# Stores of the activated values moved from ScalarE to SyncE, and the weight and factor work of two MLP stages placed anew

## The chip, the cores and the metric

One core of a Trainium2 chip runs the whole program. The metric is the device time of one execution in microseconds. Engines are called PE (TensorE), DVE (VectorE), ACT (ScalarE), POOL (GpSimd) and SP (SyncE); SP issues DMAs and computes nothing. ACT can issue DMAs too, in its own order of instructions.

## The reference

Attention with a summed key-value product, then a gated MLP with RMS norm, then a second MLP, all in float32:

```python
q_s = softmax(q, axis=-1); k_s = softmax(k, axis=2)       # 8 x 8 heads, 576 x 64
kv = einsum('bhsd,bhse->bhde', k_s, v)
x = einsum('bhsd,bhde->bhse', q_s, kv)                    # as 4608 x 512
xn = x / rms * rms_g
x = (silu(xn @ w_gate) * (xn @ w_val)) @ w_out            # 512 -> 1536 -> 512
h = x @ w_in                                              # 512 -> 2048
return (h * sigmoid(1.702 * h)) @ w_out2                  # 2048 -> 512
```

The weights arrive as 64-bit floats and are decoded to float32 on the chip.

## The kernel before

Every product runs as three matmuls: both operands are split into a rounded part and the rest (a copy on ACT, then a subtraction on DVE or POOL), and high x high, high x low and low x high are summed (`PASSES`, line 488).

The order of all instructions is written out by hand (`tc.manual_schedule()`, line 729). Each engine works its own list in that order, and the semaphores that order the engines among themselves are derived from the tiles: who writes a tile waits for the readers of what stood in that buffer before. A pool with `bufs=n` has n buffers per tag.

**GLU stage** (to line 863). Nine tiles of 512 tokens, 36 slots each. A slot is one product of 12 matmuls: gate, value, output, in turn for 12 blocks. Small jobs hang at slots. In the last tile `todo` (lines 803 to 820) is a list of (earliest slot, job), of which up to three are done per slot (line 856): the weight sets 0 to 3 of the next stage are loaded, summed and split, then the first unit's tokens are loaded (`x2_load`), summed and split. The four accumulators are evicted at the end by ACT through the `ev` tiles (`store_x2`, line 528).

**Input stage** (lines 866 to 921). The second MLP runs each product in seven instead of eight block products: sums of blocks are formed first (`sums`, line 548), each of the seven operands p is split, and the seven products are combined. A unit is 768 tokens; there are six (`NUNIT`), `END` is the last. A unit has four rounds (`in_round`, line 617) over two weight sets each, and a round has seven passes p in `ORDER` (1, 6, 2, 7, 5, 4, 3), a pass being 2 x 6 matmuls of 384 columns. So a unit has 28 passes, counted 0 to 27 from its start; `put2(i, t, fn)` hangs a job behind pass t of unit i, and `put_set(i, t, steps, lag, each)` hangs the load of a weight set at t, its sums at t + lag and its seven splits, `each` per pass, from t + lag + 1. PSUM has 8 banks; a round uses three per set. p = 2 goes into the bank of p = 1 and must wait until ACT has copied p = 1 out (`c1`, line 649); p = 7 and 4 go into the bank of p = 6, p = 3 into that of p = 5, and the additions on DVE (lines 652, 657, 661) must come between. After its addition each result passes through `gelu` (line 623): an activation on ACT into one of 12 `h` tiles, and a store to DRAM, issued by ACT (line 625).

Beside the products of unit 0 the sets 4 to 7 are prepared, all through the one tile `aside`, 5 passes apart (line 889). In units 0 to 4 the next unit's tokens are loaded into the two `raw` tiles (passes 10 and 12), summed (16 and 18) and split in two halves of channels c for each p (passes 20 to 27, lines 891 to 901). The factors of the last two p (4 and 3) have single buffers (`xg`, 4 tiles), the other ten come out of 12 `xf` tiles. In the last unit the sets 0 to 5 of the output weights are prepared in the `raw` tiles (line 902).

**Output stage** (lines 924 to 1015). Nine groups g of 512 tokens by eight sets m; step k = 8 g + m. A step is 42 matmuls of 256 columns into seven banks, p in the order 1, 6, 7, 5, 3, 4, 2. Its operand `uf` is loaded (`u2_load(k + 6)`), summed (`u2_sums`) and split (`u2_split(k + 2)`: a copy on ACT of 1792 columns, the sums of k + 3 and the subtraction on DVE) some steps ahead. Sets 6 and 7 are prepared through the single tile `y` at k = 0 to 2 and 4 to 6 (line 942), with the sums on POOL. In the last step of a group the seven banks are combined into `y` through the tiles `d1`, `d2`, `d3` (lines 986 to 1006), and ACT issues the stores at the next step (`store_out`, line 670).

The buffers of a stage lie where those of the stage before lay, and a new tile waits for the old ones under it (`reuse_waits="tile"`).

Of the kernel before, what the change touches and what calls it, by code (L numbers as in the profile page):

```python
# [8 lines left out]
F32 = mybir.dt.float32  # L9
# [11 lines left out]
def attention_glu_mlp(  # L21
# [595 lines left out]
    def in_round(i, q, after):  # L617
# [5 lines left out]
        def gelu(m, k, dst, src):  # L623
            nc.scalar.activation(dst, src, AF.Gelu_apprx_sigmoid)  # L624
            nc.scalar.dma_start(out=u2_d[i][m][:, k], in_=dst)  # L625
# [44 lines left out]
    def store_out(first, y):  # L670

        done = 0
        while done < P:
            b, o = divmod(first + done, S)
            rows = sum(halves_of(b), [])
            while o >= size(rows[0]):
                o -= size(rows.pop(0))
            m = min(P - done, size(rows[0]) - o)
            if rows[0] < R - 1:
                dst = out[b * S : b * S + FULL].rearrange("(p r) e -> r p e", p=P)[rows[0]]  # L680
            else:
                dst = out[b * S + FULL : (b + 1) * S]
            nc.scalar.dma_start(out=dst[o : o + m, :], in_=y[done : done + m, :])
            done += m
# [44 lines left out]
    with tc.manual_schedule():  # L729
# [74 lines left out]
        for j in range(NTILE):  # L804
            if j + 1 == NTILE:
# [16 lines left out]
            for slot in range(SLOTS):  # L822
# [49 lines left out]
        for p in ORDER[5:]:  # L872
            for c in range(2):
                x2_split(0, p, c)
# [14 lines left out]
        for n in range(4):  # L889
            put_set(0, 5 * n, weight_steps("2i", 4 + n, nc.gpsimd, aside_tile), 2, 3)  # L890
        for i in range(END):
            for c in range(2):
                put2(i, 10 + 2 * c, lambda i=i, c=c: x2_load(i + 1, c))
                put2(
                    i, 16 + 2 * c,
                    lambda i=i, c=c: sums(xraw2[i + 1, c], "B", (nc.vector,) * 4),
                )

            for p, t in zip(ORDER, (20, 21, 22, 23, 24, 26, 27)):
                for c in range(2):  # L900
                    put2(i, t, lambda i=i, p=p, c=c: x2_split(i + 1, p, c))
        for m, t in enumerate((1, 3, 10, 13, 17, 20)):
            put_set(END, t, weight_steps("2o", m, nc.gpsimd), (5, 6, 3, 3, 3, 3)[m])
        put2(END, 0, lambda: u2_load(0))
        put2(END, 18, lambda: u2_sums(0))
        put2(END, 25, lambda: u2_load(1))
# [5 lines left out]
        put2(END, 25, free_x)  # L912
        put2(END, 26, lambda: u2_split(0))
# [14 lines left out]
        def y_tile():  # L928
            return dpool.tile([P, 8, Q], F32, tag="y", bufs=1, name="y")

        for k in range(2, 4):
            u2_load(k)
        for t in sorted(t for i, t in beside):
            for fn in beside.pop((END, t)):
                fn()
# [4 lines left out]

        work = {}
        for m, k in ((6, 0), (7, 4)):
            a = weight_steps("2o", m, nc.gpsimd, y_tile, nc.gpsimd)
            work[k], work[k + 1], work[k + 2] = a[:1], a[1:5], a[5:]
        stores = []
        for k in range(NT // T * NSET):
# [16 lines left out]
            if last:  # L963
# [3 lines left out]
                c1, u2, u3 = (  # L967
                    dpool.tile([P, 512], F32, tag=n, bufs=1, name=n) for n in ("d1", "d2", "d3")
                )
            for p in (1, 6, 7, 5, 3, 4, 2):  # L970
# [19 lines left out]
                if p == 1:  # L990
                    nc.scalar.activation(c1, t, AF.Copy)
                elif p == 6:
                    add(half(u2), half(c1))
                elif p == 7:
                    add(half(u3), half(u2))
                elif p == 5:
                    add(y2[:, :, 0:Q], half(u3))
                    add(half(u2), half(u2))
                    u2_split(k + 2)
                    u2_load(k + 6)  # L1000
                elif p == 3:
                    add(y1[:, :, 0:Q], half(u2))
                elif p == 4:
                    add(y2[:, :, Q:T], half(u3))
                else:
                    add(y1[:, :, Q:T], half(c1))
            if last:
                for i in range(2):
                    for h, y in ((0, y2), (1, y1)):
                        stores.append(  # L1010
                            lambda i=i, h=h, y=y, g=g: store_out(first_token(g, i, h)[2], y[:, i, :])
                        )
# [45 lines left out]
```

## Time and profile before

| | |
|---|---|
| median of 3 runs | 1845.46 us (1845.21 to 1847.75) |
| the profiled execution | 1846.57 us, of which the span from first to last instruction is 1844.8 |
| PE, PEld | 1748.1 us (95%), 1545.6 us (84%) |
| DVE | 1197.5 us (65%) |
| ACT | 781.7 us (42%) |
| POOL | 388.8 us (21%) |
| granted TensorE clock | 0.985 of full speed on the mean |
| DMA | 186.30 MB, 101 GB/s on the mean |

PEld is the loading of weights into TensorE, beside the matmuls. The granted clock of a stretch is a share of 2.4 GHz; the clock has two levels, 1.2 and 2.4 GHz, so 0.92 is a mixture. Input stage and output stage run from 1086 to 1460 and from 1463 to 1838 us. The row of a timeline gives the start, the length, the engine and line, the number of instructions merged, and in brackets how long the engine stood before them and what ended that.

### The profile page before, as it was taken

What the parts mean: (1) busy time and instruction counts of PE and PEld (TensorE: products, weight loads), DVE (VectorE), ACT (ScalarE), POOL (GpSimd) and SP (SyncE); (2) the same over time, 40 slices, a digit from 0 to 9 for tenths busy, and PEclk for the clock granted to TensorE, in tenths of its full rate; (3) what the DMA queues carried; (4) which work ended last, traced back from release to release, by engine and by line L of the source; (5) the groups of instructions that cost most, each with busy time, mean ns of one, the idle gap of its engine ahead of it and who ended that gap; (6) DMA issues with size and microseconds to landing.
All of it is one profiled execution on the core that took longest, in us unless ns stands there. A gap on an engine that the chain in (4) does not pass through costs nothing.

```text
span 1844.8 us, 26565 instructions
## 1 busy us (share of the span) xinstructions
PE 1748.1 (95%) x10092; PEld 1545.6 (84%) x10092; DVE 1197.5 (65%) x2021; ACT 781.7 (42%) x1304; POOL 388.8 (21%) x360
## 2 busy tenths in 40 slices
PE   5777899999999999999999998999999899999998
PEld 4555788888888888888888888999999889999998
DVE  7999875766757567564324355455545877777775
ACT  4565544444435444443212344344435533333332
POOL 4666512121121121211111613000001540000000
PEclk9898999999999999999999999999999999999999
DMA  5344332332223323120001124443343544444442
GB/s 156 120 141 123 115 97 71 96 88 79 75 69 96 90 78 109 35 81 1 23 1 46 32 100 141 137 138 133 110 155 137 177 131 135 136 126 126 128 125 80
DMA packets 201744, 186.30 MB, mean 101 GB/s; under 512 B 58256, under 2 KB 183184, under 8 KB 201616
## 3 DMA queue, kind: packets, MB, share of 16 engines
q1 hardware_dynamic: 163536, 127.96, 23.3%
q10 hardware_dynamic: 38080, 56.64, 8.6%
q8 instruction: 79, 1.29, 0.3%
q14 instruction: 49, 0.40, 0.1%
HBM read 119.54 MB, written 65.01 MB: 100 GB/s over the span
## 4 chain that ended last, share of the span: by engine, by line
PE 77%; DVE 10%; ACT 4%; issue 3%; DMA 2%; ACTq 1%; SPq 1%; POOL 1%; DVEq 0%; POOLq 0%
PE ps_gv L493 29%; PE ps_out L975 19%; PE ps_acc L493 15%; PE ps_in L639 11%; ACT h L624 2%; ACTq L625 1%; PE ps_att L370 1%; ACT xf L553 1%; PE ps_att L399 1%; DVE h L661 1%; DVE w L151 1%; DVE raw L550 1%; DVE raw L151 1%; DVE xf L554 1%; DVE u L509 1%
## 5 line engine op out<-in xcount | busy, mean ns | idle before, releaser
L975 PE MATMUL ps_out<-w2o,uf 128*128 128x256 f32 x3024 | 368.3, 285 | 9.1 <-POOL w2o L554 4.3
L975 PEld LDWEIGHTS ps_out<-w2o,uf 128*128 128x128 f32 x3024 | 367.0, 194 | 10.5 <-POOL w2o L554 4.8
L639 PE MATMUL ps_in<-xf,w2i 128*128 128x384 f32 x2016 | 357.4, 337 | 19.0 <-ACT h L649 12.8
L639 PEld LDWEIGHTS ps_in<-xf,w2i 128*128 128x128 f32 x2016 | 351.9, 189 | 24.6 <-ACT h L649 16.2
L493 PE MATMUL ps_acc<-u,wo 128*128 128x512 f32 x1296 | 327.6, 402 | 7.2 <-POOL wo L161 6.3
L493 PE MATMUL ps_gv<-xs,wg 128*128 128x512 f32 x1296 | 322.3, 397 | 7.7 <-POOL wg L161 6.2
L493 PE MATMUL ps_gv<-xs,wv 128*128 128x512 f32 x1296 | 318.1, 394 | 0.0
L493 PEld LDWEIGHTS ps_gv<-xs,wg 128*128 128x128 f32 x1296 | 243.3, 190 | 63.1 <-POOL wg L161 8.3
L493 PEld LDWEIGHTS ps_acc<-u,wo 128*128 128x128 f32 x1296 | 243.8, 193 | 60.4 <-POOL wo L161 7.6
L493 PEld LDWEIGHTS ps_gv<-xs,wv 128*128 128x128 f32 x1296 | 240.4, 189 | 48.1 <-POOL wv L161 0.8
L161 POOL TENSOR_TENSOR wo<-raw,wo 128x512 fp32r<-128x512 f32 x108 | 142.2, 1317 | 494.5 <-ACT wo L160 476.5
L827 ACT ACTIVATE s<-ps_gv 128x512 f32<-128x512 f32 x108 | 64.6, 598 | 428.6 <-PE ps_gv L493 428.5
L833 DVE TENSOR_TENSOR s<-s,ps_gv 128x512 f32<-128x512 f32 x108 | 73.9, 684 | 203.4 <-PE ps_gv L493 185.5
L624 ACT ACTIVATE h<-h 128x384 f32<-128x384 f32 x144 | 75.6, 525 | 136.6 <-DVE h L661 118.3
L157 POOL TENSOR_TENSOR w<-w,stage 128x512 int32<-128x512 int32 x56 | 73.5, 1313 | 220.1 <-DVE w L154 70.9
L550 DVE TENSOR_TENSOR raw<-raw 128x256 f32<-128x256 f32 (+1 forms) x236 | 106.8, 494 | 10.7 <-DMA raw<-w2d 6.8
L661 DVE TENSOR_TENSOR h<-h,ps_in 128x384 f32<-128x384 f32 x144 | 76.7, 552 | 41.4 <-PE ps_in L639 40.0
L719 ACT ACTIVATE uf<-raw 128x1792 fp32r<-128x1792 f32 x36 | 61.1, 1701 | 84.4 <-PE ps_out L975 61.9
L554 POOL TENSOR_TENSOR w2o<-raw,w2o 128x256 fp32r<-128x256 f32 x42 | 32.7, 808 | 286.2 <-ACT w2o L553 283.5
L721 DVE TENSOR_TENSOR uf<-raw,uf 128x1792 fp32r<-128x1792 f32 x36 | 73.4, 2038 | 19.0 <-ACT uf L719 18.9
L510 DVE TENSOR_TENSOR u<-s,u 128x512 fp32r<-128x512 f32 x108 | 83.2, 770 | 3.7
L360 DVE TENSOR_REDUCE qs<-qe 128x10 f32<-128x640 f32 x32 | 26.2, 820 | 84.8 <-ACT qe L354 84.7
(138 smaller groups left out, 1843.1 us busy)
## 6 DMA issues: line engine op xcount, KB each, us to landing
u<-h ACTq DMA_DIRECT2D x192, 192.0 KB, 1.9
stage<-in_moe_w_out_dram SPq DMA_DIRECT2D x28, 512.0 KB, 3.6
raw<-u SPq DMA_DIRECT2D x24, 512.0 KB, 4.3
x<-ev ACTq DMA_DIRECT2D x36, 256.0 KB, 2.0
stage<-in_moe_w_in_dram SPq DMA_DIRECT2D x16, 512.0 KB, 3.6
w2d<-w SPq DMA_DIRECT2D x32, 256.0 KB, 3.4
out_dram<-y ACTq DMA_DIRECT2D x32, 256.0 KB, 4.1
v_sb<-in_v_dram SPq DMA_DIRECT2D x60, 128.0 KB, 3.1
```

The lines of the kernel that those rows point to most:

```text
L157: return lambda: nc.gpsimd.tensor_tensor(dst, dst, lo, op=ALU.add)
L161: nc.gpsimd.tensor_tensor(dst[:, 1, :], src, f(dst[:, 0, :]), op=ALU.subtract)
L493: nc.tensor.matmul(t, w(a), x(e), start=first and i == 0, stop=last and i == 2)
L510: nc.vector.tensor_tensor(u[:, 1, :], s, f(u[:, 0, :]), op=ALU.subtract)
L550: engine.tensor_tensor(raw[:, o], raw[:, a], raw[:, b], op=op)
L624: nc.scalar.activation(dst, src, AF.Gelu_apprx_sigmoid)
L639: nc.tensor.matmul(t, w[:, a, s, c * P : (c + 1) * P], xfac[i, p, c][:, e, :], start=p in (1, 6, 5) and c == 0 and k == 0, stop=c == 1 and ...
L661: nc.vector.tensor_tensor(v, v, t, op=ALU.add)
L721: nc.vector.tensor_tensor(w[:, 1], raw, f(w[:, 0]), op=ALU.subtract)
L827: nc.scalar.activation(s, tg, AF.Silu)
L833: nc.vector.tensor_tensor(s, s, tv, op=ALU.mult)
L975: nc.tensor.matmul(t[:, i * Q : (i + 1) * Q], u[:, a, LEFT[p] - 1, i * P : (i + 1) * P], w[:, e, m % 2, :], start=m == 0 and i == 0 and n ...
```

## The change

It has these parts:

- The store in `gelu` is issued by SP.
- End of the GLU stage: both pairs of weight sets and the first unit's sums come two to three slots earlier, and from slot 33 on two jobs are done per slot. The splits of p = 4 and 3 for unit 0 no longer stand ahead of the input stage.
- Four PSUM tiles that nothing uses are allocated before the first round, so that it begins with the fifth bank.
- Sets 4 and 6 go through `aside`, sets 5 and 7 through the `raw` tiles, with other passes for load, sums and splits.
- The splits of p = 4 and 3 move from passes 26 and 27 of a unit to passes 0 and 2 of the next.
- In the last unit set 2 goes through `aside`, the passes of all six sets change, u2_load(0) moves from pass 0 to 16, and the first `uf` split from pass 26 to the front of pass 25, without the sums of the next one.
- Output stage: two `y` tiles; the loads of sets 6 and 7 are issued at its start. The tiles `d1` to `d3` are replaced by quarters of `y`. The stores of a group go out in another order, and those of the last group partly on SP, the `y2` half two additions earlier.

```diff
         def gelu(m, k, dst, src):
             nc.scalar.activation(dst, src, AF.Gelu_apprx_sigmoid)
-            nc.scalar.dma_start(out=u2_d[i][m][:, k], in_=dst)
+            nc.sync.dma_start(out=u2_d[i][m][:, k], in_=dst)
...
-    def store_out(first, y):
+    def store_out(first, y, queue=nc.scalar):
...
-    def u2_split(k):
+    def u2_split(k, ahead=True):
...
         nc.scalar.activation(w[:, 0], raw, AF.Copy)
-        u2_sums(k + 1)
+        if ahead:
+            u2_sums(k + 1)
...
-                for q, gate in enumerate((12, 22)):
+                for q, gate in enumerate((10, 20)):
...
-                    todo.append((31, lambda c=c: sums(xraw2[0, c], "B", (nc.vector,) * 4)))
+                    todo.append((28, lambda c=c: sums(xraw2[0, c], "B", (nc.vector,) * 4)))
...
-                for _ in range(3):
+                for _ in range(3 if slot < 33 else 2):
...
-        for p in ORDER[5:]:
-            for c in range(2):
-                x2_split(0, p, c)
+        for _ in range(4):
+            pools["ps"].tile([P, 512], F32, tag="bank", bufs=8, name="ps_none")
...
-        for n in range(4):
-            put_set(0, 5 * n, weight_steps("2i", 4 + n, nc.gpsimd, aside_tile), 2, 3)
-        for i in range(END):
...
+        put_set(0, 0, weight_steps("2i", 4, nc.gpsimd, aside_tile), 2)
+        put_set(0, 3, weight_steps("2i", 5, nc.gpsimd))
+        put_set(0, 6, weight_steps("2i", 6, nc.gpsimd, aside_tile), 4)
+        put_set(0, 4, weight_steps("2i", 7, nc.gpsimd), 9)
+        for i in range(-1, END):
+            if i >= 0:
                 for c in range(2):
+                    t = 10 + (7 if i == 0 else 2) * c
+                    put2(i, t, lambda i=i, c=c: x2_load(i + 1, c))
+                    t = 16 + (4 if i == 0 else 2) * c
...
+            for p, t in zip(ORDER, (20, 21, 22, 23, 24, 28, 30)):
+                for c in range(2):
+                    if t >= 28:
+                        put2(i + 1, t - 28, lambda i=i, p=p, c=c: x2_split(i + 1, p, c))
+                    elif i >= 0:
+                        put2(i, t, lambda i=i, p=p, c=c: x2_split(i + 1, p, c))
+        last = [weight_steps("2o", m, nc.gpsimd, aside_tile if m == 2 else raw_tile) for m in range(6)]
+        for m, load, t in ((0, 1, 6), (1, 3, 9), (2, 1, 12), (3, 10, 15), (4, 13, 19), (5, 18, 22)):
+            put_set(END, load, last[m], t - load)
+        put2(END, 16, lambda: u2_load(0))
+        put2(END, 21, lambda: u2_sums(0))
+        put2(END, 23, lambda: u2_load(1))
...
-        put2(END, 25, free_x)
-        put2(END, 26, lambda: u2_split(0))
+        beside[END, 25].insert(0, free_x)
+        beside[END, 25].insert(1, lambda: u2_split(0, False))
+        put2(END, 25, lambda: u2_load(2))
...
-            return dpool.tile([P, 8, Q], F32, tag="y", bufs=1, name="y")
+            return dpool.tile([P, 8, Q], F32, tag="y", bufs=2, name="y")
...
+        u2_load(3)
+        work = {}
+        for m, k in ((6, 1), (7, 3)):
+            a = weight_steps("2o", m, nc.gpsimd, y_tile, nc.gpsimd)
+            a[0]()
+            work[k], work[k + 1] = a[1:5], a[5:]
...
-                c1, u2, u3 = (
-                    dpool.tile([P, 512], F32, tag=n, bufs=1, name=n) for n in ("d1", "d2", "d3")
-                )
+                c1, u2, u3 = y1[:, :, Q:T], y1[:, :, 0:Q], y2[:, :, Q:T]
+                end = g == NT // T - 1
...
                 elif p == 4:
-                    add(y2[:, :, Q:T], half(u3))
+                    add(u3, u3)
+                    if end:
+                        for i in range(2):
+                            store_out(first_token(g, i, 0)[2], y2[:, i, :], nc.sync)
...
+                for h, y in ((0, y2), (1, y1)):
+                    for i in range(2):
+                        if h or not end:
+                            queue = nc.sync if end and i else nc.scalar
...
```

## Rows read from the trace of the kernel before

**Rows 1.** Busy time by stretch, instructions, granted TensorE clock, DMA share.

```profile
1086.22:1108.86 22.64, 22.63 (x120) 22.31 (x120) 9.60 (x20) 11.72 (x25) 5.74 (x8) 0.92 0.40 136
1223.72:1284.29 60.57, 58.92 (x336) 58.15 (x336) 31.86 (x63) 26.17 (x55) 0.00 (x0) 1.00 0.38 131
1465.50:1502.66 37.16, 37.06 (x293) 36.66 (x293) 30.36 (x45) 15.42 (x17) 11.37 (x13) 0.96 0.55 169
1520.00:1837.64 317.64, 317.63 (x2643) 317.25 (x2641) 243.01 (x356) 107.97 (x69) 0.00 (x0) 1.00 0.40 123
```

**Rows 2.** Waits of PE, 1083 to 1163.5: total, times, longest.

```profile
PE ps_in L639 <- ACT h L649: 6.2, 3, 2.7
PE ps_in L639 <- ACT ev L530: 2.4, 1, 2.4
PE ps_in L639 <- DVE h L661: 2.4, 1, 2.4
PE ps_in L639 <- DVE h L652: 1.4, 1, 1.4
```

**Rows 3.** Timeline of PE: start, us, what, count, idle before and releaser.

```profile
1080.40 0.47 PE L493 MATMUL ps_acc<-u,wo 128*128 128x512 f32 x1 [0.69 <-DVE u L509]
1144.48 16.41 PE L639 MATMUL ps_in<-xf,w2i 128*128 128x384 f32 x84 [2.68 <-ACT h L649]
...
1163.18 58.90 PE L639 MATMUL ps_in<-xf,w2i 128*128 128x384 f32 x336 [2.29 <-ACT h L649]
1223.72 58.92 PE L639 MATMUL ps_in<-xf,w2i 128*128 128x384 f32 x336 [1.65 <-ACT h L649]
...
1463.44 0.50 PE L975 MATMUL ps_out<-w2o,uf 128*128 128x256 f32 x2 [3.18 <-ACT uf L719]
1465.50 37.16 PE L975 MATMUL ps_out<-w2o,uf 128*128 128x256 f32 x293 [1.56 <-DVE uf L721]
1505.14 2.05 PE L975 MATMUL ps_out<-w2o,uf 128*128 128x256 f32 x12 [2.47 <-POOL w2o L554]
1508.99 328.65 PE L975 MATMUL ps_out<-w2o,uf 128*128 128x256 f32 x2717 [1.80 <-POOL w2o L554]
```

**Rows 4.** Stores of line 625: issue min/median/max in ns; landing.

```profile
L625 ACTq DMA_DIRECT2D u<-h x192: 325/326/1175, 1093.8 to 1467.4; - x192
...
DMA to landing us min/median/max: 1.8/1.9/5.8
```

**Rows 5.** x2 loads: issues, KB, us to landing; twelve on SP's timeline.

```profile
raw<-x SPq DMA_DIRECT2D x16, 192.0 KB, 3.5
...
1162.96 6.75 SPq L606 DMA_DIRECT2D raw<-x  x12
```

**Rows 6.** Timeline of ACT, a gelu in unit 5.

```profile
1411.69 0.53 ACT L624 ACTIVATE h<-h 128x384 f32<-128x384 f32 x1 [3.02 <-DMA u<-h]
```

**Rows 7.** Timeline of DVE, the sums of set 5 in unit 0.

```profile
1108.16 1.56 DVE L550 TENSOR_TENSOR aside<-aside 128x256 f32<-128x256 f32 x4 [4.96 <-POOL w2i L554]
```

**Rows 8.** Timeline of ACT across the start of unit 3.

```profile
1282.93 0.94 ACT L553 ACTIVATE xf<-raw 128x384 fp32r<-128x384 f32 x2 [0.40 <-PE ps_in L639]
1283.77 0.85 ACT L649 ACTIVATE h<-ps_in 128x384 f32<-128x384 f32 x2
```

**Rows 9.** Timelines of ACT and DVE at the change of stage.

```profile
1461.71 1.68 ACT L719 ACTIVATE uf<-aside 128x1792 fp32r<-128x1792 f32 x1
...
1463.42 2.02 DVE L721 TENSOR_TENSOR uf<-aside,uf 128x1792 fp32r<-128x1792 f32 x1 [0.26 <-ACT uf L719]
1465.37 1.01 DVE L661 TENSOR_TENSOR h<-h,ps_in 128x384 f32<-128x384 f32 x2
1466.29 3.02 DVE L550 TENSOR_TENSOR raw<-raw 128x256 f32<-128x256 f32 x8
```

**Rows 10.** Timeline of POOL, the sums of set 6.

```profile
1480.16 2.95 POOL L550 TENSOR_TENSOR y<-y 128x256 f32<-128x256 f32 x4 [17.28 <-DMA y<-w2d]
```

**Rows 11.** Timeline of all engines, the last stores.

```profile
1838.42 2.79 ACTq L683 DMA_DIRECT2D out_dram<-y  x5
```

More of the change, by code (lines that the diff above doesn't have):

```diff
@@ L682, in store_out @@
                 dst = out[b * S + FULL : (b + 1) * S]
-            nc.scalar.dma_start(out=dst[o : o + m, :], in_=y[done : done + m, :])
+            queue.dma_start(out=dst[o : o + m, :], in_=y[done : done + m, :])
             done += m
@@ L887, in put_set @@
                 put2(i, t + lag + 1 + n // each, fn)
-        for n in range(4):
-            put_set(0, 5 * n, weight_steps("2i", 4 + n, nc.gpsimd, aside_tile), 2, 3)
-        for i in range(END):
[L892 to L896, printed above, removed]
-                )
-            for p, t in zip(ORDER, (20, 21, 22, 23, 24, 26, 27)):
-                for c in range(2):
[L901 to L906, printed above, removed]
+        put_set(0, 0, weight_steps("2i", 4, nc.gpsimd, aside_tile), 2)
[4 more added lines that the diff above has]
+            if i >= 0:
+                for c in range(2):
+                    t = 10 + (7 if i == 0 else 2) * c
+                    put2(i, t, lambda i=i, c=c: x2_load(i + 1, c))
+                    t = 16 + (4 if i == 0 else 2) * c
+                    put2(
+                        i, t, lambda i=i, c=c: sums(xraw2[i + 1, c], "B", (nc.vector,) * 4)
+                    )
+            for p, t in zip(ORDER, (20, 21, 22, 23, 24, 28, 30)):
[10 more added lines that the diff above has]
+        put2(END, 23, lambda: u2_load(1))
         def free_x():
@@ L928, in y_tile @@
         def y_tile():
-            return dpool.tile([P, 8, Q], F32, tag="y", bufs=1, name="y")
[L931 to L935, printed above, removed]
+            return dpool.tile([P, 8, Q], F32, tag="y", bufs=2, name="y")
+        assert not beside
+        u2_load(3)
[4 more added lines that the diff above has]
+            work[k], work[k + 1] = a[1:5], a[5:]
         u2_sums(1)
@@ L939, in attention_glu_mlp @@
             u2_load(k)
[L941 to L944, printed above, removed]
         stores = []
@@ L990, in attention_glu_mlp @@
                 if p == 1:
-                    nc.scalar.activation(c1, t, AF.Copy)
+                    nc.scalar.activation(c1, half(t), AF.Copy)
                 elif p == 6:
-                    add(half(u2), half(c1))
+                    add(u2, c1)
                 elif p == 7:
-                    add(half(u3), half(u2))
+                    add(u3, u2)
                 elif p == 5:
-                    add(y2[:, :, 0:Q], half(u3))
-                    add(half(u2), half(u2))
+                    add(y2[:, :, 0:Q], u3)
+                    add(u2, u2)
                     u2_split(k + 2)
@@ L1001, in attention_glu_mlp @@
                 elif p == 3:
-                    add(y1[:, :, 0:Q], half(u2))
+                    add(u2, u2)
                 elif p == 4:
-                    add(y2[:, :, Q:T], half(u3))
+                    add(u3, u3)
+                    if end:
+                        for i in range(2):
+                            store_out(first_token(g, i, 0)[2], y2[:, i, :], nc.sync)
                 else:
-                    add(y1[:, :, Q:T], half(c1))
+                    add(c1, c1)
             if last:
[L1008 to L1012, printed above, removed]
+                for h, y in ((0, y2), (1, y1)):
+                    for i in range(2):
+                        if h or not end:
+                            queue = nc.sync if end and i else nc.scalar
+                            stores.append(
+                                lambda i=i, h=h, y=y, g=g, queue=queue: store_out(
+                                    first_token(g, i, h)[2], y[:, i, :], queue
+                                )
+                            )
         for fn in stores:
```

1 line of the change is left out of this document (removed).

## The prediction

> **What bounds the kernel now.** I read the busy time by stretch first [rows 1]. PE is busy in nearly all of a steady unit of the input stage (58.92 of 60.57 us) and in all of the output stage after 1520. There 336 matmuls of 384 columns take 58.92 us, 0.175 us each, and 2643 matmuls of 256 columns take 317.63 us, 0.120 each, 5.04 for the 42 of a set. The change leaves those 2016 and 3024 matmuls as they are, so 353 + 363 us of PE stay, and what can move is the time in which PE stands or runs slowly. Then the waits of PE in the first unit [rows 2] and its timeline [rows 3] show where. Of the stretches in [rows 1] the one from 1086.22 has a granted clock of 0.92 and the one from 1465.5 of 0.96, a mixture of the levels 2.4 and 1.2 GHz; each starts right behind a gap. The price of that is in the same rows: 120 matmuls took 22.64 instead of 21.0 us (1.6 lost), 293 took 37.16 instead of 35.2 (2.0 lost).
>
> What PE loses from 1080 on:
> - (a) 0.69 us at 1080, waiting for a u split on DVE [rows 3];
> - (b) 2.42 us for the last eviction (ev) before the input stage [rows 2], and 1.6 of slow clock behind it;
> - (c) in unit 0, 2.4 and 1.4 us for DVE and 6.2 for the copy of line 649, of which 2.29 are unit 1's start [rows 2, 3]: 7.7. The 84 matmuls from 1144.48 took 16.41 instead of 14.7 us, 1.7 more. 9.4;
> - (d) at the starts of units 1 to 5, 2.29, three times 1.65, and 1.64 [rows 3] (of four alike the first stands there): 8.9;
> - (e) at the change of stage 3.18 and 1.56 us for uf, with two matmuls between, and 2.0 of slow clock: 7.0;
> - (f) before set 7, 2.47 and 1.80 for w2o on POOL; the 12 matmuls between took 2.05 instead of 1.4, and the 2717 behind took 328.65 instead of 326.0, so 2.6 + 0.6: 7.5;
> - (g) the tail behind the last matmul.
>
> **The change part by part.**
>
> *Stores on SyncE.* ACT issues 192 stores of 0.326 us [rows 4]; they go, 63 us of ACT time, 2.6 per round of 14.7. Little of it is on the path by itself: only at unit starts, in unit 0 and at the change of stage does PE wait for ACT. They now stand in SP's order, each behind its gelu and behind every load that the program puts before it. SP's own time is small: 32 stores by 0.33 and twelve x2 loads by 6.75 [rows 5] are 17 us in a unit of 60. The new cost is the head of the queue. A gelu that writes a new h tile takes the one allocated twelve before it, whose gelu and store stood about four passes (8.4 us) earlier. Less the gelu (0.53), the issue (0.33) and the landing (1.9 [rows 4]) 5.6 us are to spare. Six loads of one x2 half take 3.4 us to issue and 3.5 to land [rows 5], so a store right behind them may come up to 1.3 us too late; a store issued two passes later doesn't. The nearest row is a gelu that stood 3.02 us for a store in unit 5, where no PE gap follows [rows 6]; so I take nothing. The ends are 0 and the whole landing, 3.5 us in each of the 11 rounds that hold loads (three in unit 0, one in each of units 1 to 4, four in unit 5). They can't be below nothing, as the ACT time gained is counted in the other terms.
>
> The Trainium skill speaks against this part: "DMA: Bandwidth & Descriptors", section "Anatomy of one DMA", says that DMA engines don't wait on semaphores, the issuing sequencer does, before dispatch. By that a load that waits for its tile holds all stores behind it. The trace agrees [rows 7]: the load of set 5 wasn't issued until POOL was done. By the gelu of [rows 6] the sum below stays as it is; by the rule at its hardest, 11 landings of 3.5, all of it would be gone.
>
> *Last factors in the next unit (d).* Ahead of the copies of line 649, which must free the first bank before p = 2, ACT now has four xf splits of 0.47 and eight issues in the last round; the first copy ends 1.65 us after PE wants the bank [rows 3, 8]. After the change no split and no issue stands there: 0.94 for the last two splits and 2 x 0.33 come off at the very end, and the earlier two as much again, 3.2 against the 1.65 to 2.29 needed. The splits go behind the copies of the next unit, five passes (10 us) before their use for p = 4. Rounds inside a unit, which have that order, show no gap (336 matmuls in one piece [rows 3]). I take all 8.9; low end 5.
>
> *Banks and sums at the end of the GLU stage (a, b).* Sums three slots (8 us) earlier leave DVE free before the last u: 0.7 gained. PE's first matmul waited for the last eviction, so the first banks are those of the accumulators; with four stepped over the first round starts in others, and 2.42 and the slow clock behind it go, 4.0. Its x2 factors are ready; only p = 4 and p = 3 come later. Low end 0.
>
> *Rooms for sets 4 to 7 (c).* Today one tile serves four sets: DVE stands 4.96 us before the sums of set 5, because the load waited for POOL to finish set 4 [rows 7], and PE waits for DVE and ACT behind it. After it, sets 5 and 7 load into the x2 tiles from pass 3 and 4 on; their sums stand at 6 and 13, set 6's at 10, all three to nine passes (6 to 19 us) behind the load, for about 3.5 us of landing. What is late next is set 4: its load waits for the ev stores as before while PE starts 2.4 us sooner. Counted from PE's new start, the last ev ends at 2.4, its store lands at 4.6 (0.33 + 1.9), the load at 8.1 (3.5); sums (1.5 [rows 9]), two xf halves and the u3 add (0.5 each) end at 11.1, and PE wants that bank at five passes, 10.5: 0.7 lost. 9.4 - 0.7 = 8.7; low end 4.
>
> *Change of stage (e).* The first uf split moves one pass up. Count from PE's end of p = 5 in the last round: ACT finishes its gelus at 1.2 and uf (1.68) at 2.9, DVE's half (2.02) at 4.9 [rows 9]. PE ends p = 4 and 3 at 4.2 and stands 0.5 for the low half. DVE then has four adds (2.2), the sums of two ufs (3.0) and uf 1 (2.0): ready at 12.1, while PE wants it at 4.7 + 5.04 = 9.8. That is a new gap of 2.3 at set 1. Loss 2.8 instead of 7.0: 4.2 gained; ends 2.2 (the slow clock returns) and 7.0.
>
> *Sets 6 and 7 (f).* POOL stood 17.28 us until y was loaded [rows 10], and set 7 had to wait for set 6's tile. With two y tiles both loads are issued at the start, the sums of set 7 stand at k = 3 and it is used at k = 7, 20 us later; POOL, idle for those 17.28 us today, has 3.0 of sums and seven splits to do for each. 7.5 gained; low end 3.
>
> *Partial sums in y, stores of the tail (g).* The adds stay as many and as long; no gap stands there now, nothing gained or lost. In the last group the y2 stores go out on SP two adds earlier and the y1 stores on two queues. Five issues on ACT took 2.79 us at the end [rows 11]; now one or two do: 1.3 gained, ends 0 and 2.2.
>
> **Sum.** 0.7 + 4.0 + 8.7 + 8.9 + 4.2 + 7.5 + 1.3 = 35.3 us. The profiled execution took 1846.57 us (span 1844.8 and 1.8 around it): 1811.3. The median of before is 1.1 below it, so 1810.
>
> **The rivals.**
> 1. *Stores late by what exceeds the slack.* 1.3 us for each of the ten x2 halves, 13 us: 1823. For it: the 5.6 us are worked out without the data of the loads in front; against it: of the stores close behind loads only those of p = 3 are wanted again so soon, and [rows 6].
> 2. *The change doesn't remove the waits of unit 0 and the stage change fully.* DVE, whose sums stood 4.96 us for a load [rows 7], stays the last in unit 0 and keeps half of (c), and the short gaps that stay keep the clock low (1.6 + 1.7 + 2.0): 4.7 + 5.3 = 10 us, 1820. For it: the slow stretches all begin behind gaps of 2.4 us or more, and I forecast one of 2.3.
> 3. *Slower: the queue of SP becomes the bound.* In each of the 11 rounds with loads the gelus wait for stores that stand behind loads, PE stands for a landing (3.5) and pays 1.7 of slow clock: 11 x 5.2 = 57, and 35.3 gained: 1867. It decides from 3.2 us a round on. Against it: 17 us of SP's 60 per unit.
>
> **How the numbers follow.** Forecast 0.66 (own range 1806 to 1817), rival 1 0.13, rival 2 0.13, rival 3 0.06; 0.02 lie between, near no change. The likeliest gives 1810. With every best end the sum is 0.7 + 4.0 + 9.4 + 8.9 + 7.0 + 7.5 + 2.2 = 39.7, 1805.8. From 1805 to 1825 the range takes in rivals 1 and 2. Faster by over 0.2% (3.7 us, about what a measurement of this kernel can tell from no change) 0.92, within 0.02, slower 0.06.
>
> **What would show it.** PE's timeline without a gap at the five unit starts (d) and none before set 7 (f); the input stage starting within 0.3 us of the last output matmul of the GLU stage (b); gaps in unit 0 that sum to about 1 us with a granted clock of 1.00 (c); one gap of about 2 us at set 1 of the output stage (e). Wrong: gelus that wait for u<-h, PE waiting for ACT or DVE right behind pass 10 or 12 of a unit, or a granted clock under 1.00 in the units.

## The result, and the profile after

The changed kernel takes 1816.07 us (median of 4 runs, 1815.13 to 1816.74) beside 1845.34 us before: 0.984 of the time, with a 95% interval of 0.982 to 0.986. The forecast was 1810, the range 1805 to 1825. Its profiled execution took 1816.74 us (span 1814.9), 29.9 us of span less than before where 35.3 were forecast. The time lies in the range. The sum came out 5.4 us too large, and its terms missed by more than that in both directions. Of all runs one, of the last experiment, took 1936.97 us at a granted clock of 0.85, and no time below counts it.

PE's timeline of the kernel after, the same view as [rows 3], from the last products of the GLU stage to the last matmul:

```profile
1077.64 5.60 PE L493 MATMUL ps_acc<-u,wo 128*128 128x512 f32 x24
1085.66 349.92 PE L639 MATMUL ps_in<-xf,w2i 128*128 128x384 f32 x2016 [2.42 <-ACT ev L530]
1435.42 0.40 PE L984 MATMUL ps_out<-w2o,uf 128*128 128x256 f32 x2
1436.33 5.56 PE L984 MATMUL ps_out<-w2o,uf 128*128 128x256 f32 x42 [0.51 <-DVE uf L722]
1445.36 27.34 PE L984 MATMUL ps_out<-w2o,uf 128*128 128x256 f32 x210 [3.47 <-DVE uf L722]
1473.41 13.69 PE L984 MATMUL ps_out<-w2o,uf 128*128 128x256 f32 x112 [0.71 <-DVE uf L722]
1487.52 121.39 PE L984 MATMUL ps_out<-w2o,uf 128*128 128x256 f32 x1008 [0.42 <-DVE y L998]
1609.10 198.59 PE L984 MATMUL ps_out<-w2o,uf 128*128 128x256 f32 x1650 [0.18 <-DVE y L998]
```

The whole input stage is one piece: 2016 matmuls without a gap, where [rows 3] have gaps in unit 0 and at every unit start. The gap ahead of it is as long as before, 2.42 us. At the change of stage and behind it there are five gaps, all for DVE. From these pieces and [rows 3] the 29.9 us split by place:

| stretch | before | after | gained | forecast |
|---|---|---|---|---|
| to the first matmul of the input stage | 1086.22 | 1085.66 | 0.6 | 3.1 |
| first to last matmul of the input stage | 374.0 | 349.9 | 24.1 | 19.2 |
| from there to the last matmul | 377.4 | 372.1 | 5.3 | 11.7 |
| behind the last matmul | 7.2 | 7.2 | 0 | 1.3 |

In the forecast, (a) and the gap of (b) stand in the first line, (c), (d) and the 1.6 us of slow clock of (b) in the second, (e) and (f) in the third, (g) in the fourth.

PE's own row hides one thing. These are PE's weight loads (PEld) from 1170 to 1430 us, most of units 1 to 5: busy us, mean ns, and idle time with what ended it. Before:

```profile
L639 PEld LDWEIGHTS ps_in<-xf,w2i 128*128 128x128 f32 x1447 | 250.5, 188 | 9.8 <-ACT h L649 8.7 <-DVE h L652 1.1
```

After:

```profile
L639 PEld LDWEIGHTS ps_in<-xf,w2i 128*128 128x128 f32 x1500 | 260.0, 188 | 0.2 <-ACT h L649 0.2
```

Before, the weight loads stood 9.8 us, and the four unit starts in this window explain 4 x 1.65 = 6.6 of them. Of the other 3.2 us, 1.9 are eight short waits of 0.16 to 0.34 us inside the units, for ACT and DVE, and 1.2 stand at the unit starts, where the last matmul still runs behind its weight load. The PE row counts both as busy. That is why 336 matmuls took 58.9 us before [rows 3] and 349.92 / 6 = 58.3 after.

The stores on SP (line 625), the same view as [rows 4]:

```profile
L625 SPq DMA_DIRECT2D u<-h x192: 319/320/1359, 1091.7 to 1439.2; - x192
...
DMA to landing us min/median/max: 1.8/1.9/5.1
```

An issue takes 320 ns and a landing 1.9 us, as on ACT. Some issues stand in the queue and some landings take up to 5.1 us, but PE, with 2016 matmuls in one piece, feels none of it.

### The profile page after: what moved, and what is told of

It is laid out like the page before. It is cut to its first block, busy times and chain, and to the rows that moved or that the text cites. A ratio compares the mean times of both kernels' runs of the same rounds, so it can differ in the third digit from the quotient of the medians.

```text
span 1814.9 us, 26699 instructions
## 1 busy us (share of the span) xinstructions
PE 1742.3 (96%) x10092; PEld 1543.3 (85%) x10092; DVE 1203.9 (66%) x2017; ACT 779.9 (43%) x1304; POOL 396.1 (22%) x360
## 4 chain that ended last, share of the span: by engine, by line
PE 85%; DVE 10%; issue 2%; DMA 1%; ACT 1%; POOL 0%; SPq 0%; DVEq 0%; ACTq 0%; POOLq 0%
PE ps_gv L493 29%; PE ps_in L639 19%; PE ps_out L984 17%; PE ps_acc L493 15%; PE ps_att L370 1%; PE ps_att L399 1%; DVE uf L722 1%; DVE w L151 1%; DVE raw L151 1%; DVE raw L550 1%; DVE raw L154 1%; DVE u L509 1%; PE ps_att L449 1%; DVE y L998 0%; DVE m L316 0%
## 5 line engine op out<-in xcount | busy, mean ns | idle before, releaser
L639 PE MATMUL ps_in<-xf,w2i 128*128 128x384 f32 x2016 | 349.9, 334 | 2.4 <-ACT ev L530 2.4
L554 POOL TENSOR_TENSOR w2o<-raw,w2o 128x256 fp32r<-128x256 f32 x35 | 28.2, 843 | 275.9 <-DMA u<-h 270.1
```

The lines of the kernel that those rows point to most:

```text
L639: nc.tensor.matmul(t, w[:, a, s, c * P : (c + 1) * P], xfac[i, p, c][:, e, :], start=p in (1, 6, 5) and c == 0 and k == 0, stop=c == 1 and ...
```

## The experiments

The first five undo or isolate a part. The others test one cause each. The times of two kernels of the kind of after can be told apart from about 2 us on; where they lie closer, the rows decide.

**Stores alone on the kernel before (e1_stores_alone).**

```diff
-            nc.scalar.dma_start(out=u2_d[i][m][:, k], in_=dst)
+            nc.sync.dma_start(out=u2_d[i][m][:, k], in_=dst)
```

> The kernel before with the stores of the activated values issued by SP, nothing else. Theory A (ACT is full in the last round of a unit: 14 splits, 8 activations, 2 copies and 8 issues fill its 14.7 us, so taking away either the issues or the late splits brings the copies of line 649 in time): no gap at the five unit starts, 8.9 us gained; in unit 0 the gaps for ACT go and those for DVE (1.38, 2.40) stay; about 1830 to 1834 us. Theory B (both are needed, as the sum of the prediction had it: 0.66 of 1.65 us come off here): gaps of about 1 us stay at the unit starts, about 1838 us.

1831.61 us, 0.992 of before (0.989 to 0.995). PE's timeline:

```profile
1130.87 6.54 PE L639 MATMUL ps_in<-xf,w2i 128*128 128x384 f32 x36 [1.54 <-DVE h L661]
1138.63 302.13 PE L639 MATMUL ps_in<-xf,w2i 128*128 128x384 f32 x1740 [1.22 <-ACT h L649]
1441.77 0.51 PE L975 MATMUL ps_out<-w2o,uf 128*128 128x256 f32 x2 [1.02 <-ACT uf L719]
1446.59 7.26 PE L975 MATMUL ps_out<-w2o,uf 128*128 128x256 f32 x42 [4.31 <-DVE uf L721]
1456.48 31.87 PE L975 MATMUL ps_out<-w2o,uf 128*128 128x256 f32 x251 [2.64 <-DVE uf L721]
```

From unit 0 to the end of the input stage the matmuls run in one piece of 302 us (0.1736 us each, as in after). All five unit starts are gone without a factor having moved, and two of the gaps of unit 0 too. The stage change got longer than in [rows 3]: 1.0 + 4.3 + 2.6 us. So the one line brings half of the gain: 15.5 us against the runs of before beside it (1847.10), of 29.3.

**Last factors alone on the kernel before (e2_factors_alone).**

```diff
-            for p, t in zip(ORDER, (20, 21, 22, 23, 24, 26, 27)):
+            for p, t in zip(ORDER, (20, 21, 22, 23, 24, 28, 30)):
                 for c in range(2):
-                    put2(i, t, lambda i=i, p=p, c=c: x2_split(i + 1, p, c))
+                    put2(i + t // 28, t % 28, lambda i=i, p=p, c=c: x2_split(i + 1, p, c))
```

> The kernel before with the splits of p = 4 and 3 moved from passes 26 and 27 to passes 0 and 2 of the next unit, nothing else. Theory A: no gap at the starts of units 1 to 5, the gaps of unit 0 and the stage change as before, 8.9 us gained, about 1836 us. Theory B: gaps of 0.5 to 1 us stay, about 1840 us.

1835.85 us, 0.995 (0.992 to 0.997). PE's timeline around the last gap of unit 0 and in the units:

```profile
1145.46 236.07 PE L639 MATMUL ps_in<-xf,w2i 128*128 128x384 f32 x1344 [2.69 <-ACT h L649]
1381.85 69.17 PE L639 MATMUL ps_in<-xf,w2i 128*128 128x384 f32 x396 [0.32 <-ACT h L649]
```

This part removes the unit starts by itself too, all but one remainder of 0.32 us, and leaves unit 0 much as it was (four gaps of 8.3 us in all, 7.7 before). With the stores still on ACT a matmul takes 236.07 / 1344 = 0.1756 us, as before and not as in e1.

**After, the stores back on ACT (e3_no_stores).**

```diff
-            nc.sync.dma_start(out=u2_d[i][m][:, k], in_=dst)
+            nc.scalar.dma_start(out=u2_d[i][m][:, k], in_=dst)
```

> The changed kernel with the stores of the activated values back on ACT. Theory A: no gaps at the unit starts, as the late splits are gone; in unit 0 the weight splits and the issues meet on ACT, gaps of 1 to 4 us in all; the change of stage 1 to 2 us later: 1818 to 1822 us. Theory C (the move to SP carries most of the gain, because ACT also stands for the DMA that it issues): gaps in every unit, 1828 us or more.

1822.07 us, 0.987 (0.984 to 0.990), 6.0 us above after. PE's timeline and PEld over the same window as above:

```profile
1085.56 33.56 PE L639 MATMUL ps_in<-xf,w2i 128*128 128x384 f32 x192 [2.42 <-ACT ev L530]
1119.53 162.16 PE L639 MATMUL ps_in<-xf,w2i 128*128 128x384 f32 x924 [0.42 <-ACT h L649]
1282.19 132.24 PE L639 MATMUL ps_in<-xf,w2i 128*128 128x384 f32 x756 [0.50 <-ACT h L649]
1415.09 25.50 PE L639 MATMUL ps_in<-xf,w2i 128*128 128x384 f32 x144 [0.65 <-ACT h L649]
```

```profile
L639 PEld LDWEIGHTS ps_in<-xf,w2i 128*128 128x128 f32 x1481 | 256.3, 188 | 4.0 <-ACT h L649 2.9 <-DVE h L652 1.1
```

The three gaps are 1.6 us. The four pieces take 353.5 us, 3.5 more than the one of after: these are the short waits, with the ends of three more pieces, and with the stores on ACT they are back. So the stores act on more than gaps.

**After, the last factors back (e4_no_factors).**

```diff
-            for p, t in zip(ORDER, (20, 21, 22, 23, 24, 28, 30)):
+            for p, t in zip(ORDER, (20, 21, 22, 23, 24) + ((28, 30) if i < 0 else (26, 27))):
```

> The changed kernel with the splits of p = 4 and 3 for units 1 to 5 back at passes 26 and 27 of the unit before. Theory A: no gap at the unit starts, since ACT has no issues; 1816 to 1817 us, as the changed kernel. Theory B: gaps of about 1 us at five unit starts, 1821 us.

1817.15 us, 0.984 (0.981 to 0.987), as after by time; and the input stage stays in one piece:

```profile
1085.36 349.92 PE L639 MATMUL ps_in<-xf,w2i 128*128 128x384 f32 x2016 [2.42 <-ACT ev L530]
```

With the stores on SP the place of the last factors no longer matters. Stores and factors are two cures for the same 8.9 us, and each is enough.

**After, the sets 4 to 7 through one tile again (e5_one_room).**

```diff
-        put_set(0, 0, weight_steps("2i", 4, nc.gpsimd, aside_tile), 2)
-        put_set(0, 3, weight_steps("2i", 5, nc.gpsimd))
-        put_set(0, 6, weight_steps("2i", 6, nc.gpsimd, aside_tile), 4)
-        put_set(0, 4, weight_steps("2i", 7, nc.gpsimd), 9)
+        for n in range(4):
+            put_set(0, 5 * n, weight_steps("2i", 4 + n, nc.gpsimd, aside_tile), 2, 3)
...
-                    t = 10 + (7 if i == 0 else 2) * c
+                    t = 10 + 2 * c
...
-                    t = 16 + (4 if i == 0 else 2) * c
+                    t = 16 + 2 * c
```

> The changed kernel with sets 4 to 7 through the one tile as before (passes 0, 5, 10, 15, sums two passes later) and the second half of unit 1's tokens loaded at pass 12 and summed at 18 as before. Theory A (most of unit 0's loss came from ACT, which the stores left; the rooms are worth what was left with the stores alone moved, 1.54 + 1.22): gaps of 2 to 3 us in unit 0, 1818 to 1819 us. Theory P (the prediction: the rooms carry (c), 8.7 us): 1824 us.

1820.57 us, 0.986 (0.983 to 0.989). PE's timeline:

```profile
1084.74 43.41 PE L639 MATMUL ps_in<-xf,w2i 128*128 128x384 f32 x240 [2.42 <-ACT ev L530]
1129.26 6.52 PE L639 MATMUL ps_in<-xf,w2i 128*128 128x384 f32 x36 [1.11 <-DVE h L661]
1137.01 302.31 PE L639 MATMUL ps_in<-xf,w2i 128*128 128x384 f32 x1740 [1.23 <-ACT h L649]
```

Two gaps come back, 2.3 us, and 240 matmuls take 43.41 instead of 41.7 us, slow clock behind the gap of 2.42 (granted 0.95 from 1085.7 to 1108.3). With the stores on SP the rooms are worth those 2.3 us, not the 8.7 of term (c); the clock isn't shown to be theirs, as e8 and e11 below have 0.93 and 0.92 there with the rooms of after: most of what stood in unit 0 hung on ACT's stores.

**After, 8 instead of 12 h tiles (e6_eight_h).**

```diff
-            return pools["h"].tile([P, W], F32, tag="h", bufs=12, name="h")
+            return pools["h"].tile([P, W], F32, tag="h", bufs=8, name="h")
```

> The changed kernel with 8 instead of 12 h tiles, so that a store has some 4 us less before its tile is wanted again. Theory Q (a store stands on SP behind six x2 loads for up to 6.9 us, which 12 tiles hide): gaps of 2 to 5 us at passes 10 to 16 of every unit, PE waiting for ACT or DVE, 1830 to 1850 us. Theory N (the loads are issued so far from the stores that matter that SP's order costs nothing): no gap, 1816 us.

1815.65 us, 0.983 (0.980 to 0.986). The profile now puts 11.0 us of ACT's idle time down to stores that five gelus waited for, 2.6 us at most. One of them on ACT's timeline, first the same gelu in after and then here:

```profile
1178.57 0.49 ACT L624 ACTIVATE h<-ps_in 128x384 f32<-128x384 f32 x1 [2.63 <-PE ps_in L639]
1177.63 0.49 ACT L624 ACTIVATE h<-ps_in 128x384 f32<-128x384 f32 x1 [2.63 <-DMA u<-h]
```

It starts 92.91 us behind the stage's first matmul (1085.66 and 1084.72) in both, and in after it stood the same 2.63 us for PE. The other four start where they do in after too, within 0.01 us. So these stores landed last of what the gelus wait for, but made none of them later, and PE's piece is still 349.92 us. Rivals 1 and 3 are away from their point of decision even with a third fewer tiles.

**The first bank (e7_first_bank).** In after, the four PSUM tiles that nothing uses take no bank: the first product of the input stage has the bank of the last eviction, as before. Here one of them is written, by a DVE memset of one column:

```diff
-        for _ in range(4):
-            pools["ps"].tile([P, 512], F32, tag="bank", bufs=8, name="ps_none")
+        first_bank = pools["ps"].tile([P, 512], F32, tag="bank", bufs=8, name="ps_none")
+        nc.vector.memset(first_bank[:, 0:1], 0.0)
```

> The changed kernel with the four unused PSUM tiles replaced by one tile that DVE writes one column of. Theory F (tiles that nothing uses take no bank, so the first round still begins in the bank of the fourth accumulator, which ACT evicts last; a tile that is used takes that bank and the first pass starts in a free one): the gap of 2.42 us before the input stage goes, of which 0.5 to 1 come back at pass 5, where DVE is late because set 4 arrives no earlier: 1814 to 1814.6 us. Theory G (PE waits for ACT there in any case, because its copies stand behind the evictions): the gap goes and comes back whole at p = 2, 1816 us.

1816.64 us, 0.984 (0.981 to 0.987). PE's and DVE's timelines:

```profile
1082.65 10.59 PE L639 MATMUL ps_in<-xf,w2i 128*128 128x384 f32 x60
1095.39 339.49 PE L639 MATMUL ps_in<-xf,w2i 128*128 128x384 f32 x1956 [2.14 <-DVE h L657]
```

```profile
1090.80 1.98 DVE L550 TENSOR_TENSOR aside<-aside 128x256 f32<-128x256 f32 x4 [1.88 <-DMA aside<-w2d]
1092.70 2.08 DVE L554 TENSOR_TENSOR xf<-raw,xf 128x384 fp32r<-128x384 f32 x2
1094.70 1.01 DVE L657 TENSOR_TENSOR h<-h,ps_in 128x384 f32<-128x384 f32 x2
```

The gap at the start is gone, and five passes later 2.14 us stand in its place: DVE waits for the load of set 4, and the addition that frees PE's next bank is queued behind its sums. The prediction named this ("what is late next is set 4") and put it at 0.7.

**The first bank, and set 4 one pass later (e10_bank_and_set4).** The edit of e7, and

```diff
-        put_set(0, 0, weight_steps("2i", 4, nc.gpsimd, aside_tile), 2)
+        put_set(0, 0, weight_steps("2i", 4, nc.gpsimd, aside_tile), 3)
```

> The changed kernel with the used tile in the first bank and the sums of set 4 one pass later (3 instead of 2). Theory S (the gap came back at pass 5 because the sums of set 4, which wait for its load, stood on DVE ahead of the additions of p = 7): no gap at the start of the stage and none in unit 0, 2.4 us gained, 1813.5 to 1814 us. Theory G (some chain behind the evictions sets the start in any case): a gap of about 2 us further on, 1816 us.

1813.89 us, 0.982 (0.979 to 0.985), 2.2 us below after. PE's timeline:

```profile
1083.07 349.83 PE L639 MATMUL ps_in<-xf,w2i 128*128 128x384 f32 x2016
```

The sums of set 4 now stand behind the two additions of line 657, and neither gap is left.

**The sums ahead moved back at the change of stage (e8_sums_later).**

```diff
         u2_sums(1)
-        u2_split(1)
+        u2_split(1, False)
+        u2_sums(2)
```

> The changed kernel with the sums of operand 2 put behind the split of operand 1 at the start of the output stage. Theory H (the gap of 3.47 us at step 1 is 2.2 us of DVE waiting for the load of operand 2 and 1.55 us of its sums, ahead of the subtraction that PE waits for): the gap shrinks to about 1.5 us, the slow clock behind it goes, a gap of up to 1.7 us comes at step 2: 1812.5 to 1814.5 us. Theory I (DVE is the bound of the first steps whatever its order): the gap is only moved to step 2, 1816 us.

1817.27 us, 0.984 (0.981 to 0.987). PE's timeline of the first steps:

```profile
1436.97 0.40 PE L985 MATMUL ps_out<-w2o,uf 128*128 128x256 f32 x2
...
1445.00 5.28 PE L985 MATMUL ps_out<-w2o,uf 128*128 128x256 f32 x42 [1.56 <-DVE uf L722]
1451.16 5.30 PE L985 MATMUL ps_out<-w2o,uf 128*128 128x256 f32 x42 [0.89 <-DVE uf L722]
...
1474.96 13.70 PE L985 MATMUL ps_out<-w2o,uf 128*128 128x256 f32 x112 [0.70 <-DVE uf L722]
```

The gap of 3.47 becomes 1.56, and gaps in the next steps take the rest: from the stage's first matmul to the piece of 112 it is 37.99 us here and 37.99 in after (1435.42 to 1473.41). The granted clock behind the gap (1445.3 to 1472.7) is 1.00 here and 0.94 in after, so the slow clock of that stretch cost after nothing. PE's steps start 5.6 to 6.2 us apart there, where PE alone needs 5.04. Neither the wait for one load nor the clock sets the time; DVE is the bound until it has caught up.

**POOL kept quieter (e11_quiet_pool).** The edit of e8, and the sums of sets 6 and 7 on DVE, a step later:

```diff
-        for m, k in ((6, 1), (7, 3)):
-            a = weight_steps("2o", m, nc.gpsimd, y_tile, nc.gpsimd)
+        for m, k in ((6, 2), (7, 4)):
+            a = weight_steps("2o", m, nc.gpsimd, y_tile)
```

> The changed kernel with the sums of operand 2 behind the split of operand 1, the sums of weight sets 6 and 7 on DVE, and their work at steps 2, 3 and 4, 5 instead of 1, 2 and 3, 4. Theory H (DVE is the bound of the first eight steps because its sums take 3.6 instead of 1.55 us and its subtractions 2.56 instead of 2.02 beside POOL): gaps of 0.5 and about 1.5 us, then at most 0.7 in all up to step 8 (after the sums alone were moved: 0.5, 1.56, 0.89, 0.93, 0.27, 0.71, 0.70, 0.42), 1812.5 to 1814 us. Theory J (DVE hasn't the time for the added 3 us of sums either): gaps of 4 us or more as before, 1816 us.

1817.64 us, 0.984 (0.981 to 0.987). DVE's and POOL's timelines:

```profile
1458.61 1.54 DVE L550 TENSOR_TENSOR y<-y 128x256 f32<-128x256 f32 x4
1465.01 3.59 DVE L550 TENSOR_TENSOR ur<-ur 128x256 f32<-128x256 f32 x4
```

```profile
1462.27 6.04 POOL L554 TENSOR_TENSOR w2o<-y,w2o 128x256 fp32r<-128x256 f32 x5 [0.29 <-ACT w2o L553]
```

Four sums take 1.54 us with POOL idle and 3.59 beside its splits; a split takes 6.04 / 5 = 1.21 us beside DVE. The 14 splits stayed on POOL and DVE got eight sums more. PE's gaps are 0.51, 1.56, 1.09 and 2.96 us, so nothing was won. No run takes POOL's work out of these steps altogether.

**The last group stored in quarters (e9_quarters).** The tail of after, but each quarter of y leaves as soon as its last addition is done, one token half on SP and one on ACT:

```diff
+                def quarter(h, n):
+                    if end:
+                        for i, queue in enumerate((nc.sync, nc.scalar)):
+                            store_out(
+                                first_token(g, i, h)[2], (y2, y1)[h][:, i, :], queue,
+                                slice(n * Q, (n + 1) * Q),
+                            )
...
                 elif p == 3:
                     add(u2, u2)
+                    quarter(1, 0)
...
```

> The changed kernel with the last group stored in quarters, each pair on SP and ACT right behind the addition that ends it (after p = 5, 3, 4 and 2). Theory T (the tail is bound by the data: 1.05 MB that all begin to move at the last two additions and keep the DMA engines busy for 4 us): 0.26 MB are left behind the last addition, the span ends 1.5 to 2.5 us sooner behind PE's last matmul, 1813.5 to 1814.5 us. Theory U (the end is the fixed time of one store to land and of the program's last waits): 0 to 0.5 us, 1816 us.

1814.58 us, 0.982 (0.979 to 0.985). The last stores, first in after and then here (issue ns min/median/max, first and last start):

```profile
L683 SPq DMA_DIRECT2D out_dram<-y x4: 450/524/571, 1808.5 to 1810.6; - x4
L683 ACTq DMA_DIRECT2D out_dram<-y x1: 338/338/338, 1809.1 to 1809.1; - x1
...
DMA to landing us min/median/max: 2.9/3.4/3.5
```

```profile
L683 SPq DMA_DIRECT2D out_dram<-y x6: 466/537/587, 1807.4 to 1810.8; - x6
L683 ACTq DMA_DIRECT2D out_dram<-y x4: 338/386/512, 1807.4 to 1810.0; - x4
...
DMA to landing us min/median/max: 1.9/2.4/2.7
```

From the last matmul to the end of the span it is 5.4 us (1808.63 to 1814.0) instead of 7.2. The first stores start before the last matmul ends, and each carries half as much. The earlier start, the smaller stores and the second queue come together here; which of them gains how much isn't shown.

**What worked, together (e12_bank_set4_quarters).** The edits of e10 and e9.

> The kernel after with the used PSUM tile and the sums of set 4 at lag 3 (the kernel that took 1813.89 us) and the last group stored in quarters on two queues (1814.58 alone, tail 5.4 instead of 7.2 us). Theory U: the two act in different places, the start of the input stage and the time behind the last matmul, so they add: 1813.9 - 1.8 = about 1812 us (1811.5 to 1812.7), no gap on PE from 1083 to 1433 us and 5.4 us from the last matmul's end to the end of the span. Theory V: what is won at the start is lost at the change of stage, whose waits follow DVE and POOL rather than PE, so that only the larger gain stays: about 1814 us, with gaps of more than 4.5 us there.

1811.82 us (median of five runs, 1811.38 to 1812.38), 0.981 (0.980 to 0.982): faster than before, and than after, whose interval begins where this one ends. PE's timeline:

```profile
1082.53 349.81 PE L639 MATMUL ps_in<-xf,w2i 128*128 128x384 f32 x2016
...
1442.10 27.87 PE L984 MATMUL ps_out<-w2o,uf 128*128 128x256 f32 x210 [3.46 <-DVE uf L722]
```

The two gains add, 4.2 us below after, as theory U has it. The 3.46 us at the change of stage stay as they were.

## Why the prediction was right or wrong

The time lies in the range, in part by luck. The waits that the prediction listed in the input stage and for POOL are gone, all but the one for the eviction, and neither of the queue rivals came about. But the two largest terms came true by a cause other than the one given for them, and what was forecast too large by 10.2 us in all was offset by 4.9 us forecast too small. Term by term:

- **(a) Right.** The last 24 matmuls of the GLU stage run without the 0.69 us gap. The input stage started 0.6 us earlier and no more, as it waits for the eviction as before. (In e3 to e6, e8, e9 and e11, alike up to there, it starts between 1084.72 and 1085.88.)
- **(b) Wrong: 4.0 forecast, 1.6 gained.** The step that failed is "with four stepped over the first round starts in others". Tiles that nothing uses step over nothing, so the first round doesn't begin with the fifth bank; the gap of 2.42 us is the row of [rows 2] once more, and e7 shows that one used tile removes it. The 1.6 us of slow clock behind it are missing in after (2016 matmuls at 0.1736 us), but the change isn't shown to have done that: behind the same gap the granted clock is 0.95 in e5, 0.93 in e8 and 0.92 in e11, and 1.00 in e3, e4, e6 and e9. This 1.6 is luck. And (b) was not to be had alone: e7's 2.14 us in the place of 2.42 are three times the 0.7 charged in (c), because DVE's sums and the two xf halves take 1.98 and 2.08 us beside POOL instead of 1.5 and 1.0.
- **(c) and (d) right in size, wrong in their cause.** All 9.4 and 8.9 us are gone, with 4.2 more that no term had. The step that failed is the sentence on the stores, "little of it is on the path by itself", with nothing taken for them in the sum. By e1 the stores alone remove every unit start and two of the gaps of unit 0; by e4 the factors that got the credit for (d) can go back at no cost; by e5 the rooms are worth 2.3 us of (c). The starting point was off as well: 353 us of PE were said to stay, and some 3.5 of them were short waits for ACT and DVE, and ends of pieces, that the PE row shows as busy. The PEld rows hold them, e3 brings them back.
- **(e) Wrong in size: 4.2 forecast, hardly 1 gained.** The forecast was gaps of 0.5 and 2.3 us, 2.8 lost instead of 7.0. The gaps are 0.51 and 3.47, and the slow clock stayed, at the end that the prediction kept open: 210 matmuls took 27.34 instead of 25.2 us. The change of stage in after, DVE, POOL and SP:

```profile
1431.83 1.43 POOL L554 TENSOR_TENSOR w2o<-raw,w2o 128x256 fp32r<-128x256 f32 x2
1434.59 2.27 POOL L554 TENSOR_TENSOR w2o<-raw,w2o 128x256 fp32r<-128x256 f32 x1 [1.34 <-ACT w2o L553]
1436.89 0.53 SPq L702 DMA_DIRECT2D raw<-u  x1
1441.81 1.55 DVE L550 TENSOR_TENSOR raw<-raw 128x256 f32<-128x256 f32 x4 [2.21 <-DMA raw<-u]
1443.28 2.02 DVE L722 TENSOR_TENSOR uf<-raw,uf 128x1792 fp32r<-128x1792 f32 x1
```

  The step that failed is DVE's list of adds, sums and subtraction without a wait in it. The second sums stood 2.21 us for a load which SP could issue only at 1436.89, when POOL's last split of set 5 had freed the tile. That split took 2.27 us, beside DVE's subtraction (1434.25 to 1436.27), where the two before it took 0.72 each. So DVE had uf 1 ready 13.9 us behind PE's end of p = 5 (about 1431.4), not 12.1. But by e8 the stage takes as long without this wait and without the slow clock: what it lost is DVE's pace, under (f).
- **(f) Half right.** Both waits for POOL are gone. Small ones for DVE came, 0.71 + 0.42 + 0.18 us. The term was 0.5 us too large from the start, as 2717 matmuls at 317.63 / 2643 us are 326.5 us and not 326.0. The step that failed is that POOL's sums and splits, moved beside DVE's steps, were costed by POOL's idle time and not by what they do to DVE. DVE's steps in after, first beside POOL, the last with POOL idle:

```profile
1458.80 2.56 DVE L722 TENSOR_TENSOR uf<-aside,uf 128x1792 fp32r<-128x1792 f32 x1
1461.28 3.60 DVE L550 TENSOR_TENSOR raw<-raw 128x256 f32<-128x256 f32 x4
...
1475.28 2.02 DVE L722 TENSOR_TENSOR uf<-ur,uf 128x1792 fp32r<-128x1792 f32 x1
```

  2.56 + 3.60 is 6.2 us a step, over PE's 5.04; 2.02 + 1.55 with POOL idle is under it, and behind the last of POOL's splits (1473.95) only the gaps of 0.42 and 0.18 us are left. How the 5.3 us of the third stretch part between (e) and (f) can't be read exactly, since DVE's pace runs through both. The price stood in the trace of before: on DVE's timeline, while POOL made the splits of set 6 (1483.08 to 1490.53), four sums took 3.60 us and not the 1.5 that the prediction took from [rows 9]:

```profile
1486.32 3.60 DVE L550 TENSOR_TENSOR raw<-raw 128x256 f32<-128x256 f32 x4
```

- **(g) Wrong: 1.3 forecast, 0 gained.** The step that failed is the counting of issues alone. In before the y2 stores could already leave ahead of the last addition, and the first store starts 0.8 us behind the last matmul in both. In after four of the five last issues stood on SP, 0.52 us each, and landed in 3.4 us at the median, against 2.9 before. The end is set by the data behind the last addition; e9 starts it earlier and gains the 1.8.
- **Rivals.** 1 and 3 did not come about: 0 us of PE in after, and still 0 in e6, where no gelu starts later in the stage. The gelu of [rows 6], the prediction's reason to take nothing, was no late store either: it starts 6.10 us behind its unit's first matmul, and in units 3 and 4 the same gelu starts 6.13 and 6.12 us behind, after 3.22 us that are put down to DVE. Nothing was the right price, but that row didn't show it. The sentence of the Trainium skill on the issuing sequencer ("DMA: Bandwidth & Descriptors", "Anatomy of one DMA") agrees with the trace in kind, as stores do stand behind loads in SP's order (in after, one whose gelu ended at 1173.40 is issued at 1175.68, behind six loads); the price that was put on it at its hardest did not arise. Rival 2 came about in part, in another place: the change of stage and not unit 0. Its "DVE stays the last" is right, for POOL's sake and not for the load of set 5.

The errors: (a) and (b) together 2.5 too much, (c) and (d) with the clock 4.9 too little, (e) and (f) 6.4 too much, (g) 1.3 too much: 5.4 with the roundings.

## What to carry to other kernels

Where an in-order engine both computes and issues DMAs, cost its issues against the waits that end on it, gap by gap, and read the weight loads' idle time beside PE's: short waits hide in a row that shows PE busy. The stores and the last factors, two edits that relieve the same engine, didn't add; forecast such edits as one. A wait that the profile puts down to one cause may have had a second that ended as late: see where the same instruction starts in a unit or run without the first. Before work goes to an idle POOL, see which operations DVE runs at that time, and cost those at their rate beside POOL, which the trace may already hold.

## What the runs showed of the hardware

- **DVE and POOL slow each other.** Four sums on DVE take 1.55 us alone and 3.60 beside POOL's splits, a subtraction of 1792 columns 2.02 and 2.56, and a split on POOL 0.72 alone and 1.2 to 2.27 beside DVE. The Trainium skill ("SBUF — State Buffer", section "SBUF: two separate sides") says that the two share a pair of ports, which one instruction holds as an exclusive lock: against a POOL operation that reads SBUF, also a DVE operation with two SBUF inputs. These are such operations, and the trace agrees in that either side can lose: at 1434.25 in after DVE's subtraction kept its 2.02 us while POOL's split took 2.27, and at 1455.06 in e11 POOL's split kept 0.74 us while DVE's sums took 2.09. That it is a lock was not tested. Weighed in the prediction, this rule would have spoken against (e) and (f).
- **The same gap doesn't always cost the clock.** Behind 2.42 us for the same eviction the granted clock of the next 22.6 us was 0.92 in before [rows 1], 0.95 in e5, 0.93 in e8, and 1.00 in after. With the input stage of after unchanged in it, 2016 matmuls took 349.92 us in one profiled execution and 351.26 and 351.52 in two others (e8, e11). A term for slow clock is one that may or may not come, up to about 2 us, and where another engine is the bound, as behind the change of stage, it may cost nothing.
- **The last stores fill the DMA engines.** From 1810 to 1812 us in after the DMA engines were 96% busy and moved 272 GB/s, and moving four of the five issues to another queue gained nothing.
